# A gated linear attention feeding a gated state-space block: fourth group's alpha turned on VectorE, fourth block of the first projection moved ahead of the third group's scores

## The chip, the core and the metric

One core of a Trainium2 chip runs the whole program. Its engines work side by side and meet at semaphores: TensorE (PE in the profile; its weight loads are PEld), VectorE (DVE), ScalarE (ACT), GpSimd (POOL) and SyncE (SP), which here only issues transfers. Each engine works through its own instructions in the order in which they were written. The metric is the device time of one execution in microseconds; the kernel before takes 270.24 us in the median of three runs (270.16 to 270.40).

## What is computed

Two blocks, one feeding the other. The first is a gated linear attention over 4 batches, 8 heads, 768 steps and 48 channels. The second is a gated state-space block with 384 model channels and 512 inner ones.

```python
# first block, for each batch and head
for t in range(S):                       # S = 768
    state = alpha[t][:, None] * state + outer(k[t], v[t])
    y[t] = q[t] @ state
x = y.transpose(0, 2, 1, 3).reshape(4, 768, 384)

# second block
val, gate = split(x @ w_in)              # 512 and 512
h[t] = exp(A_log)[0] * h[t - 1] + val[t]   # along the steps, elementwise
out = (gate * sigmoid(gate) * h) @ w_out
```

## The kernel before, in words

**Groups.** The steps of a batch are cut into three groups of 256, so there are twelve groups, counted m or n = 0 to 11. The loop at the end of `fast` runs over n. In round n it makes the second block of group n (written with n) and the first block of group m = n + 1 (written with m), and it prepares q, k and alpha of the group behind that. Rounds 0 and 1 have an order of their own, written out by hand; from round 2 on the order repeats. The change lies in rounds 0 and 1. The schedule is manual: what stands first in the code is first on its engine.

**Turning q, k and alpha.** They come from memory with steps on the partitions and are needed with channels on the partitions. Two ways are in the code. `load_steps` fetches a group in two transfers, and `turned` then turns it on TensorE, either with a real transpose (L702, L703, for the groups and names in `turned_by_transpose`) or with a matmul against the identity (L707); ScalarE copies the result out of PSUM (`copy_turned`, L714; `alphas(m)` does all this for alpha). `load_raw` fetches a group in four transfers, arranged as squares of 32 partitions, and one VectorE instruction turns all of it (`turn`, L600). Groups 1 to 3 use the first way for alpha, later ones the second; q and k use the second from group 3 on. Both ways write into the same raw tile of each name: `load_steps` into one half of it by the parity of m, `load_raw` across both halves.

**First block of a group.** Turned alpha gives a running product P (L635) and its counterpart V (L654), two scans on VectorE over 1028 elements. `scaled_q` and `scaled_k` (L610, L619) multiply q by P and k by V. `scores` (L798) multiplies them on TensorE in blocks of 64 steps, `masks` (L808 for the first three groups, L813 later) puts the causal mask on them on VectorE and ScalarE copies the rest. `values` (L834) multiplies by v, `states` (L866) makes each block's contribution to the state, `add_banks` (L894) sums them on VectorE, `carried` (L847) adds what the state brings, and `join` moves the outcome into xT, the input of the second block: two ScalarE copies (L960, L961), eight small transfers half on SyncE's queue and half on GpSimd's (L963), and two ScalarE copies more (L966). `third(m)` is carried, values, carried, join.

**Second block of a group.** `project(n, cc)` is one of four blocks of the first projection: 128 value channels and 128 gate channels from xT and w_in (L988, twelve records on TensorE), a scan along the steps on VectorE (L995), and silu on ScalarE (L1006). It returns the product of the two as a function to be called later (L1008); with `late` the scan too is called later. `output` (L1022) is the second projection for groups 0 and 1.

**Weights.** w_in comes as four units, w_out as two halves, in 64-bit numbers. `load_w` and `load_w_out` fetch the bits on SyncE's queue. `low` (ScalarE, L543), `high` (VectorE, L549 and L551) and `add_low` (GpSimd, L556) turn them into 32-bit numbers; `convert` is all three. `load_w_out(0)` is issued behind a ScalarE instruction (L1218) that touches its buffer.

**PSUM.** Four banks (`mm0` to `mm3`) are handed out by `bank()` in the order of the string `taken`; every block of a projection, every second half of scores and every turned half takes from it.

**The order around the change.** Round 0 ends: block (0,2), with values and states of group 1 between its two halves; the load of w_out's first half; `alphas(3)`; `third(1)`; w_out's second half, q of group 3, alpha of group 4, v of group 3; the four scalings of group 2. Round 1 begins: scores and masks of group 2, block (0,3), the product of block (0,2), P of group 3, the scan of block (0,3), values and states of group 2, the products of blocks (0,0), (0,1), (0,3), block (1,0), both halves of w_out converted, block (1,1), the turn of k of group 3, `third(2)`, and so on.

Of the kernel before, what the change touches and what calls it, by code (L numbers as in the profile page):

```python
# [346 lines left out]
def fast(  # L347
# [22 lines left out]
    nc = tc.nc  # L370
# [24 lines left out]
    GP = GC + 1  # L395
# [6 lines left out]
    def load_raw(name, m, engine):  # L402
        if m >= N:
            return
        b, g = divmod(m, NG)
        src = srcs[name]
        to = raws[name][:, 0:4 * ROW].rearrange("p (h x) -> p h x", h=4)
        for i in range(2):
            for odd in range(2):
                n = ROW - 16 - 16 * odd  # L410
                engine.dma_start(
                    out=to[ds(64 * i + 32 * odd, 32), :, 0:n],
                    in_=src[b, ds(4 * i, 4), ds(g * GC, GC), :]
                    .rearrange("h (c j) d -> c h (j d)", c=32)[:, :, ds(32 * odd, n)])

    def steps_of(name, m):
        return raws[name][:, ds(m % 2 * (2 * ROW + 16), 2 * ROW + 16)]

    def load_steps(name, m, engines):
        b, g = divmod(m, NG)  # L420
        for i in range(2):
            engines[i % len(engines)].dma_start(
                out=steps_of(name, m)[:, ds(i * ROW, ROW)],
                in_=srcs[name][b, ds(4 * i, 4), ds(g * GC, GC), :].rearrange("h (c j) d -> c h (j d)", c=32))
# [34 lines left out]
    def load_w_out(half, engine):  # L459
        engine.dma_start(  # L460
            out=wobits[half].rearrange("p cc n two -> p cc (n two)"),
            in_=moe_w_out.bitcast(U32)[ds(2 * C * half, 2 * C)].rearrange("(cc p) n -> p cc n", p=C))
# [20 lines left out]
    als = [const.tile([C, 4 * GP + 1], FP32, name=f"al{i}") for i in range(2)]  # L483
# [74 lines left out]
    def convert(i):  # L558
        if i not in lows:
            low(i)  # L560
        high(i)
        add_low(i)
# [30 lines left out]
    def by_place(t):  # L593
        return t[:, 0:4 * GP].rearrange("p (h t) -> p h t", h=4)
# [4 lines left out]
    def turn(name, to):  # L599
        nc.vector.transpose(out=by_runs(to).rearrange("p h c j -> p h j c"),  # L600
                            in_=raws[name][:, 0:4 * ROW].rearrange("p (h j d) -> p h j d", h=4, d=D)
                            [:, :, :, 0:32])
# [58 lines left out]
    def products(m):  # L661
# [17 lines left out]

    taken = iter("0321032103231023" "1023102310231023" "102310231023" "10"
                 "23012301" "230132" "01230123" "012310" "23012301" "230132" "01230123" "012310"
                 "23012301" "230132" "01230123" "012310" "23012301" "230132" "01230123" "012310"
                 "23012301" "0132" "01320132")
# [6 lines left out]
    def bank_pair(tag=None):  # L692
        return [bank(tag and f"{tag}{i}") for i in range(2)]

    turned_by_transpose = ((0, "k"), (1, "a"), (1, "k"), (1, "q"), (3, "a"))

    def turned(m, name, js, t, by_transpose=None):
        raw = steps_of(name, m)
# [69 lines left out]
    def alphas(m):  # L768
        turn_over(m, "a", by_place(als[m % 2])[:, :, 1:GP])
# [17 lines left out]
    def scores(m, cs=range(G)):  # L787
        Zk, Zq = Zks[m], Zqs[m % 2]
        for c in cs:
            scs.setdefault(m, []).append(bank_pair(None if c else "s"))  # L790
            if not c or not m:
                sts.setdefault(m, []).extend(scs[m][c])
            for p in range(4):
                for h in range(2):
                    u = 2 * c + h
                    for i in range(2):
                        rows = ds(64 * i, D)
                        nc.tensor.matmul(scs[m][c][i][ds(L * h, L), ds(p * (L + D), L + D)],  # L798
                                         Zk[rows, c, p, ds(h * L, L)], Zq[rows, u, p],
                                         start=True, stop=True, skip_group_check=True)  # L800
# [351 lines left out]
    nc.scalar.activation(raws["a"][0:1, 0:1], sums[3][0:1, 0, 0:1], AF.Copy)  # L1152
    load_steps("a", 2, [nc.sync])
    load_w(units[2], nc.sync)
    for name in "kqa":
        load_steps(name, 2 + (name == "a"), [nc.sync])
    load_w(units[3], nc.sync)
    load_v(1, nc.sync)
    P = scan_P(1)
# [23 lines left out]
    def third(m):  # L1183
        if m < N:
            carried(m, (1,))
            values(m, False)
            carried(m, (0, 2, 3))
            return join(m, [nc.sync, nc.gpsimd])

    late = (1,)  # L1190
    for n in range(N):
        m = n + 1
        if n == 0:
# [14 lines left out]
            V = scan_V(2, P)  # L1208
            low(3)
            convert(3)  # L1210
            load_raw("k", 3, nc.sync)
            junk(1)
            def across_and_states():
# [3 lines left out]
            f2 = project(n, 2, between=across_and_states)  # L1217
            nc.scalar.activation(wobits[0][0:1, 0, 0, 0:1], minus[0:1], AF.Relu)  # L1218
            load_w_out(0, nc.sync)
            alphas(3)  # L1220
            third(m)
            load_w_out(1, nc.sync)
            for name in "qa":
                load_raw(name, 3 + (name == "a"), nc.sync)
            load_v(3, nc.sync)
            for c in range(G):
                scaled_k(2, tk, V, c)
                scaled_q(2, tq, P, c)
        elif n == 1:
            scores(m)  # L1230
            masks(m)
            h3, f3 = project(0, 3, True)
            f2()
            P = scan_P(3)
            h3()
            values(m, True)
            st = states(m)
            add_banks(m, st)
            for f in fs_late:
                f()  # L1240
            f3()
            f0 = project(n, 0)
            convert(4)
            junk(2)
            low(5)
# [11 lines left out]
            f2 = project(n, 2)  # L1257
# [4 lines left out]
            f3 = project(n, 3)  # L1262
# [6 lines left out]
        else:  # L1269
# [13 lines left out]
            f0 = project(n, 0)  # L1283
# [20 lines left out]
            f2 = project(n, 2)  # L1304
# [8 lines left out]
            f3 = project(n, 3)  # L1313
# [102 lines left out]
```

## Time and profile before

| | us |
|---|---|
| median of three runs (lowest, highest) | 270.24 (270.16, 270.40) |
| the profiled execution | 270.68 |
| its span | 269.0 |

The span is the stretch from the first to the last recorded instruction of one execution; every start time below counts from its beginning. In the chain of waits each row is a piece of the work that ended last, followed back from the end: start, length, engine, tile and line. In a timeline a row is a start, a length, an engine, a line, an operation with what it writes and reads, and in brackets how long the engine stood idle just before and what ended that. SPq is SyncE's queue: its rows are the issue of a transfer, and the rows with KB give the median time from issue to landing. Matmul durations overlap, so lengths on TensorE are taken from the chain, where pieces do not.

### The profile page before, as it was taken

Reading aid. Unit: us, or ns where it says so; the run is one execution under the profiler, and the core shown is the slowest. Engines: PE = TensorE matmul, PEld = TensorE weight load, DVE = VectorE, ACT = ScalarE, POOL = GpSimd, SP = SyncE. Lnnn points to the kernel's source line nnn. Section 1 sums busy time; section 2 is a strip of 40 time slices with the busy share of each in tenths; the row PEclk is TensorE's granted clock in tenths of the full one; section 3 lists DMA queues with packets and bytes.
Section 4 is the critical chain, followed back from the end, with each engine's and each line's share of the span. In section 5 each row is a group of like instructions: output and inputs, shape, how many; then the busy total and the mean of one; then the engine's idle time right before and its main releaser. Section 6 shows DMA issues by size and latency. Waiting matters only on the chain.

```text
span 269.0 us, 9976 instructions
## 1 busy us (share of the span) xinstructions
PE 263.0 (98%) x4168; PEld 230.2 (86%) x4168; DVE 233.5 (87%) x316; ACT 111.6 (41%) x270; POOL 165.3 (61%) x185
## 2 busy tenths in 40 slices
PE   7989999999999999999999999999999999999995
PEld 5978889886688988988988988988988989988974
DVE  7978898996999999999999999999999998883440
ACT  4666776281242631632543533524524515314011
POOL 8222304093267998996985995996886987646000
PEclk9999999999999999999999999999999999999999
DMA  5938974796993659559687478569588501201201
GB/s 173 316 117 281 296 172 139 210 225 159 243 220 90 138 159 231 119 140 229 133 227 170 107 207 184 113 173 219 128 210 172 144 3 29 75 3 37 70 7 59
DMA packets 52304, 41.19 MB, mean 153 GB/s; under 512 B 27392, under 2 KB 50944, under 8 KB 52256
## 3 DMA queue, kind: packets, MB, share of 16 engines
q1 hardware_dynamic: 49328, 37.34, 56.1%
q0 software_dynamic: 1536, 2.20, 3.1%
q10 hardware_dynamic: 1392, 0.99, 1.3%
q8 instruction: 34, 0.56, 0.9%
q14 instruction: 14, 0.11, 0.1%
HBM read 32.54 MB, written 4.72 MB: 139 GB/s over the span
## 4 chain that ended last, share of the span: by engine, by line
PE 96%; DMA 2%; issue 0%; ACTq 0%; ACT 0%
PE mm L988 48%; PE mm L1064 16%; PE y L834 4%; PE y L847 4%; PE mm L1022 4%; PE s L798 4%; PE mm L798 3%; PE s L866 3%; PE mm L707 2%; PE mm L1377 2%; DMA raw_q<-in_q_dram 2%; PE mm L702 2%; PE mm L703 1%; PE y L918 1%; PE mm L750 1%; PE y L926 1%
## 5 line engine op out<-in xcount | busy, mean ns | idle before, releaser
L988 PE MATMUL mm<-xT,w_in 128*128 128x256 f32 x576 | 129.4, 382 | 0.0
L988 PEld LDWEIGHTS mm<-xT,w_in 128*128 128x128 f32 x576 | 107.9, 190 | 16.0 <-issue 0.5
L1006 ACT ACTIVATE sg<-mm 128x256 f32<-128x256 f32 x48 | 18.4, 383 | 88.9 <-PE mm L988 88.9
L1008 POOL TENSOR_TENSOR f_last<-sg,hh 128x256 f32<-128x256 f32 x36 | 28.8, 806 | 26.1 <-ACT sg L1006 22.6
L886 POOL TENSOR_TENSOR sum<-sum,dS 128x192 f32<-128x192 f32 x30 | 39.3, 1310 | 3.0 <-ACT dS L874 1.4
L635 DVE TENSOR_TENSOR_SCAN P<-al,lower 128x1028 f32<-128x1028 f32 x12 | 30.5, 2541 | 0.3
L995 DVE TENSOR_TENSOR_SCAN hh<-a_dec,hh,mm 128x256 f32<-128x256 f32 x32 | 23.3, 728 | 8.4 <-PE mm L988 8.2
L654 DVE TENSOR_TENSOR_SCAN V<-al,ends 128x1028 f32<-128x1028 f32 x12 | 28.5, 2375 | 0.4
L963 POOL DMA_DIRECT2D xT<-yst x44 | 22.6, 518 | 5.4 <-ACT yst L960 4.0
L556 POOL TENSOR_TENSOR w_in<-w_in,wr 128x768 int32<-128x768 int32 x4 | 7.3, 1820 | 26.3 <-DVE wbits L1143 9.3
L1064 PE MATMUL mm<-wide,wr 128*128 128x192 f32 x108 | 20.8, 327 | 0.0
L600 DVE STREAM_TRANSPOSE k<-raw_k 128x1024 f32<-128x1024 f32 x9 | 18.5, 2053 | 0.0
L600 DVE STREAM_TRANSPOSE q<-raw_q 128x1024 f32<-128x1024 f32 x9 | 18.2, 2026 | 0.0
L1064 PEld LDWEIGHTS mm<-wide,wr 128*128 128x128 f32 x108 | 18.0, 190 | 0.0
L874 ACT ACTIVATE dS<-s 128x384 f32<-128x384 f32 (+1 forms) x18 | 7.4, 461 | 24.4 <-PE s L866 24.4
L818 POOL TENSOR_TENSOR AK<-AK,mask 128x512 f32<-128x512 f32 x9 | 13.7, 1520 | 5.9 <-ACT AK L814 5.7
L600 DVE STREAM_TRANSPOSE al<-raw_a 128x1024 f32<-128x1024 f32 x8 | 16.4, 2045 | 0.0
L619 DVE TENSOR_TENSOR Zk<-k,V 128x1024 f32<-128x1024 f32 (+1 forms) x14 | 15.8, 1128 | 0.1
L1064 PE MATMUL mm<-w_out,f_last 128*128 128x192 f32 x72 | 15.6, 339 | 0.0
L610 DVE TENSOR_TENSOR Zq<-q,P 128x1024 f32<-128x1024 f32 (+1 forms) x14 | 15.2, 1083 | 0.0
L847 PEld LDWEIGHTS y<-Zq,sum 48*64 48x64 f32 x656 | 11.6, 134 | 3.5 <-issue 3.0
L834 PE MATMUL y<-AK,v 64*64 64x64 f32 x352 | 14.5, 221 | 0.0
(188 smaller groups left out, 503.7 us busy)
## 6 DMA issues: line engine op xcount, KB each, us to landing
v<-in_v_dram SPq DMA_DIRECT2D x22, 192.0 KB, 3.6
out_dram<-o_sb SPq DMA_DIRECT2D x22, 192.0 KB, 2.7
raw_k<-in_k_dram SPq DMA_DIRECT2D x18, 184.0 KB, 4.6
raw_q<-in_q_dram SPq DMA_DIRECT2D x18, 184.0 KB, 4.7
raw_k<-in_k_dram SPq DMA_DIRECT2D x18, 176.0 KB, 4.9
raw_q<-in_q_dram SPq DMA_DIRECT2D x18, 176.0 KB, 4.7
wbits<-in_moe_w_in_dram SPq DMA_DIRECT2D x8, 384.0 KB, 5.7
raw_a<-in_alpha_dram SPq DMA_DIRECT2D x16, 184.0 KB, 3.6
```

The lines of the kernel that those rows point to most:

```text
L600: nc.vector.transpose(out=by_runs(to).rearrange("p h c j -> p h j c"), in_=raws[name][:, 0:4 * ROW].rearrange("p (h j d) -> p h j d", h=4, ...
L635: nc.vector.tensor_tensor_scan(out=P, data0=al[:, 0:4 * GP], data1=lower.rearrange("p h t -> p (h t)"), initial=0.0, op0=ALU.mult, op1=ALU ...
L654: nc.vector.tensor_tensor_scan(out=V[:, ::-1], data0=al[:, 1:4 * GP + 1][:, ::-1], data1=ends.rearrange("p h t -> p (h t)")[:, ::-1], init ...
L798: nc.tensor.matmul(scs[m][c][i][ds(L * h, L), ds(p * (L + D), L + D)], Zk[rows, c, p, ds(h * L, L)], Zq[rows, u, p], start=True, stop=True ...
L834: nc.tensor.matmul(ys[m][i][ds(64 * s, 64), e, ds(c * C + h * L, L)], v_sb[rows, c, 4 * i + p, :], As[i][rows, c, p, :], start=across and ...
L847: nc.tensor.matmul(ys[m][i][ds(64 * s, 64), e, ds(u * L, L)], Ss[j][rows, p, :], Zqs[m % 2][rows, u, p, D:], start=False, stop=True, skip_ ...
L886: nc.gpsimd.tensor_add(Ss[j][:, :, 0:D], Ss[j - 1][:, :, 0:D], part)
L963: engines[n % len(engines)].dma_start(out=xT[to, a], in_=st[rows, i, e])
L988: nc.tensor.matmul((pv, pg)[vg], w_ins[cc][:, kk, vg, :], xT[:, kk, :], start=(kk == 0), stop=(kk == NK - 1))
L995: nc.vector.tensor_tensor_scan(out=hh, data0=a_dec[:, cc:cc + 1].to_broadcast([C, GC]), data1=pv, initial=prev_h[cc][:, GC - 1:GC] if n % ...
L1008: f = lambda: engine.tensor_mul(fs[n][cc], sg, hh)
L1064: nc.tensor.matmul(o, a[:, k], b[k] if type(b) is list else b[:, k], start=start and k == 0, stop=k == KC - 1, skip_group_check=True)
```

## The change

It does three things together. Alpha of group 3 is fetched by `load_raw` and turned on VectorE by `turn` in round 1, between scores and masks of group 2, instead of fetched by `load_steps` and turned on TensorE in round 0; alpha of group 4, which takes the same raw tile, is fetched behind that turn. Block (0,3) of the first projection goes from behind the scores of group 2 to ahead of them, into round 0 behind `third(1)`; the product of block (0,2) and the scan of block (0,3) go ahead of the scores. Block (1,0) takes the place behind the masks, ahead of values and states of group 2. The string of banks has two entries fewer and its start is renamed to fit.

```diff
-    taken = iter("0321032103231023" "1023102310231023" "102310231023" "10"
+    taken = iter("3012301230102310" "2310231023102310" "2310231023" "10"
...
-    turned_by_transpose = ((0, "k"), (1, "a"), (1, "k"), (1, "q"), (3, "a"))
+    turned_by_transpose = ((0, "k"), (1, "a"), (1, "k"), (1, "q"))
...
     load_steps("a", 2, [nc.sync])
     load_w(units[2], nc.sync)
-    for name in "kqa":
-        load_steps(name, 2 + (name == "a"), [nc.sync])
+    for name in "kq":
+        load_steps(name, 2, [nc.sync])
     load_w(units[3], nc.sync)
...
             convert(3)
+            load_raw("a", 3, nc.sync)
             load_raw("k", 3, nc.sync)
...
             load_w_out(0, nc.sync)
-            alphas(3)
             third(m)
+            h3, f3 = project(n, 3, True)
             load_w_out(1, nc.sync)
-            for name in "qa":
-                load_raw(name, 3 + (name == "a"), nc.sync)
+            load_raw("q", 3, nc.sync)
             load_v(3, nc.sync)
...
         elif n == 1:
+            f2()
+            h3()
             scores(m)
+            turn("a", by_place(als[1])[:, :, 1:GP])
+            load_raw("a", 4, nc.sync)
             masks(m)
-            h3, f3 = project(0, 3, True)
-            f2()
+            f0 = project(n, 0)
             P = scan_P(3)
-            h3()
             values(m, True)
             st = states(m)
             add_banks(m, st)
             for f in fs_late:
                 f()
             f3()
-            f0 = project(n, 0)
             convert(4)
```

## The prediction, made before the changed kernel ran

> **What bounds the kernel now.** I read the page's span and busy shares first, then the chain of waits in order of time, then the timelines of the engines beside it.
>
> ```profile
> span 269.0 us, 9976 instructions
> PE 263.0 (98%) x4168; PEld 230.2 (86%) x4168; DVE 233.5 (87%) x316; ACT 111.6 (41%) x270; POOL 165.3 (61%) x185
> PE 96%; DMA 2%; issue 0%; ACTq 0%; ACT 0%
> ```
>
> The chain that ends last is 96% TensorE, so a microsecond taken off TensorE's order of work shortens the run, as long as nothing then arrives late. This is that chain over the stretch that the change rewrites (start, length, line, count):
>
> ```profile
> 40.88 0.11 PE mm L702
> ...
> 42.63 0.39 PE y L847 x16
> ...
> 44.19 0.77 PE s L798 x32
> 44.96 0.77 PE mm L798 x32
> 45.72 2.79 PE mm L988 x12
> 48.51 0.62 PE y L834 x32
> ...
> 49.84 5.38 PE mm L988 x24
> 55.22 0.39 PE y L847 x16
> ...
> 64.72 2.59 PE mm L988 x12
> 67.31 5.16 PE mm L1022 x16
> 72.47 0.93 PE s L798 x32
> ```
>
> Every piece starts where the one before it ends: TensorE waits for nobody here. From 40.88 to 42.63 it turns alpha 3 (L702 and L703); 45.72 is block 3 of group 0's projection, 49.84 blocks 0 and 1 of group 1's.
>
> **What goes.** The 16 transposes leave TensorE: 42.63 - 40.88 = 1.75 us. What follows them, the join's matmuls, keeps its 0.39 us start, since a 128-row matmul stands ahead of it either way (the piece at 55.22 has the same 0.39 behind the projection).
>
> **What moves.** The order becomes join work of group 1, block (0,3), scores, block (1,0), values and states, block (1,1). The same matmuls run, but the wide ones are no longer together. Two blocks in a row take 5.38 us, one alone behind small matmuls 2.79, so splitting them costs 2 x 2.79 - 5.38 = 0.20. Scores behind a wide matmul start with 0.93 instead of 0.77 (72.47 against 44.19): 0.16. **The sum on TensorE:** -1.75 + 0.20 + 0.16 = -1.39 us, if nothing is late.
>
> The new times on the old clock, from these lengths: join work 40.88 to 42.44; block (0,3) to 45.23; scores (0.93 + 0.77) to 46.93; block (1,0) to 49.72; values and states (49.84 - 48.51 = 1.33) to 51.05; block (1,1) to 53.84, where before it ended at 55.22. Now each input at its new time.
>
> VectorE and GpSimd, in their timelines:
>
> ```profile
> 39.79 1.82 POOL L556 TENSOR_TENSOR w_in<-w_in,wr 128x768 int32<-128x768 int32 x1 [6.21 <-DVE wr L551]
> 40.12 1.61 DVE L894 TENSOR_TENSOR sum<-s,sum 128x192 f32<-128x192 f32 x4
> 43.45 0.68 DVE L610 TENSOR_TENSOR Zq<-q,P 128x512 f32<-128x512 f32 x1
> 45.01 0.42 DVE L808 TENSOR_TENSOR A<-s,mask 128x256 f32<-128x256 f32 x1 [0.88 <-PE s L798]
> 54.12 4.25 POOL L556 TENSOR_TENSOR w_out<-w_out,wr 128x768 int32<-128x768 int32 x2 [6.93 <-ACT wr L543]
> 55.30 1.40 DVE L1008 TENSOR_TENSOR f_last<-sg,hh 128x256 f32<-128x256 f32 x1
> 66.06 0.75 DVE L995 TENSOR_TENSOR_SCAN hh<-a_dec,hh,mm 128x256 f32<-128x256 f32 x1 [2.50 <-PE mm L988]
> 70.14 0.41 DVE L1008 TENSOR_TENSOR f_last<-sg,hh 128x256 f32<-128x256 f32 x1
> 70.47 2.02 DVE L600 STREAM_TRANSPOSE al<-raw_a 128x1024 f32<-128x1024 f32 x1
> 72.34 2.04 DVE L600 STREAM_TRANSPOSE k<-raw_k 128x1024 f32<-128x1024 f32 x1
> ```
>
> Block (0,3) needs w_in 3, whose last addition ends at 39.79 + 1.82 = 41.61; its new start is 42.44, 0.8 us of room. The join work needs the sums, four additions of 0.4 us from 40.12: the first is there at 40.5 (wanted 40.88), the third at 41.3 (wanted at about 42.2).
>
> VectorE's added turn of alpha 3 costs 1.87 us, by the distance of the two turns at 70.47 and 72.34. It is hidden by idle time. VectorE now waits 0.88 us before the masks and 2.50 us before the scan of block (1,3), and for nothing that the profile shows between them. New: it comes out of the scaling at 44.13, takes the product of block 2 (about 0.4) and the scan of block (0,3) (0.66) at once, then the turn, then four masks of 0.36, until 48.4. TensorE wants the masks at 49.72, 1.3 us later. The stretch from 45.01 to 63.56 (66.06 less the wait of 2.50) is 18.55 us long; begun at 44.13 and lengthened by 1.87 it ends at 64.55. The scan behind it could start at 66.06 - 1.39 = 64.67. So the added work fits to a tenth of a microsecond, and the wait of 2.50 us is used up. Behind it there is room once more: the product at 70.14 ends at 70.55, while the last quarter of the output projection that reads it begins 12/16 into the 5.16 us from 67.31, at 71.18. That 0.6 us would not shrink. GpSimd's two additions for w_out, from 54.12 to 58.37, wait for VectorE too: its part for them comes up to 1.87 - 0.88 = 0.99 later, so they end between 58.37 and 59.36. The first output projection starts at 64.72 - 5.16 = 59.56, now 1.39 sooner at 58.17, and reads the second half of w_out in its third product of eight, 4/16 of 5.16 later, at 59.46: 0.1 to 1.1 us of room. I cost all this at nothing; without the two idle stretches the turn would be 1.87 us on the path.
>
> The rest of the moved block is its silu on ScalarE and its scan. They free its pair of PSUM banks for block (1,0) by about 45.7 (45.23 and a product's 0.4), before 46.93.
>
> ScalarE loses two copies of al and gains nothing but order. SyncE's queue and the transfers:
>
> ```profile
> 25.05 1.18 SPq L422 DMA_DIRECT2D raw_a<-in_alpha_dram  x2
> 28.00 5.82 SPq L441 DMA_DIRECT2D v<-in_v_dram  x4
> 34.85 1.91 SPq L411 DMA_DIRECT2D raw_k<-in_k_dram  x4
> raw_k<-in_k_dram SPq DMA_DIRECT2D x2, 184.0 KB, 3.5
> DMA packets 192, 0.24 MB, mean 245 GB/s; under 512 B 21, under 2 KB 192, under 8 KB 192
> 41.41 0.39 SPq L460 DMA_DIRECT2D wobits<-in_moe_w_out_dram  x1
> wobits<-in_moe_w_out_dram SPq DMA_DIRECT2D x1, 768.0 KB, 4.5
> 44.86 3.17 SPq L963 DMA_DIRECT2D xT<-yst  x4
> 47.45 0.58 SPq L963 DMA_DIRECT2D xT<-yst  x1
> xT<-yst SPq DMA_DIRECT2D x1, 48.0 KB, 1.9
> 57.50 4.85 SPq L963 DMA_DIRECT2D xT<-yst  x4
> L963 POOL DMA_DIRECT2D xT<-yst x44: 501/510/544, 45.1 to 247.5; - x44
> ```
>
> The two early loads of alpha 3 (2 x 192 KB, 25.05) go, so what stands behind them, w_in 3 and v, is issued 1.2 us sooner. In their place four square loads (2 x 184 + 2 x 176 = 720 KB) are issued ahead of raw_k, from about 32.6. With the time of raw_k's own squares, 3.5 us, doubled for the v packets in front, they land before 41; the turn wants them at 45.1. The bytes grow by 336 KB, 1.4 us at the 245 GB/s that the queue moved from 38 to 39, and the queue stands still between raw_k's landing (the last of four issues starts at about 36.3, and 3.5 more: 39.8) and 41.41. The load of alpha 4 moves behind v 3 and behind the turn at 47; its reader turns at 70.47, now about 69: covered by 15 us. Behind its wait in SyncE's queue stand only the moves of the next join (57.50).
>
> The one input that comes nearer is **xT of group 1**. Now SyncE's last move for it starts at 47.45 and lands at 49.35; TensorE started on it at 49.84 and needs the last third of it 0.20 + 2 x 0.43 = 1.06 later. In the new order the join work ends 1.75 us earlier, so do the copies, and the moves, if nothing holds them: landing at 47.6. Block (1,0) starts at 46.93 and needs the last third at 47.99. Room 0.4 us, where it was 1.5. What could hold them is the load of the first half of w_out, 768 KB, issued at 41.41 as now and landed at 45.9: the first move would be issued 1.7 us behind it instead of 3.45. Bounds: nothing lost, or the landing at 49.35 as before, 1.36 us lost. The nearest row is the next join at 57.50, with four issues in 4.85 us instead of 3.17: the first at 44.86 - 1.75 = 43.11, the last starting at 43.11 + 4.85 - 0.58 = 47.38, and 1.9 to land give 49.3 too. I take nothing lost: w_out's load ends at 45.9, and SyncE's four moves hold 128 KB, 0.5 us of the queue at 245 GB/s, so that even all behind it they fit before 47.99.
>
> **The sum.** The profiled execution took 270.68 us with a span of 269.0: new 270.68 - 1.39 = 269.29, span 267.6. It lies 0.44 above the median of the runs, 270.24; from that median 268.85.
>
> **The rivals.** *xT late (B).* The moves wait behind the w_out load and land near 49.35: up to 1.36 us is given back, 268.85 to 270.2, the middle 269.5. For it: the row at 57.50. Against it: the moves are 48 KB and less, and the load ends at 45.9.
>
> *VectorE the bound (C).* The fit to a tenth above breaks when products run beside GpSimd's additions: one more 1.40 us product in place of 0.41, less the 0.1 or 0.6 us of room, costs 0.4 to 0.9: 269.5. Against it: the stretch already holds one such product (55.30).
>
> [...]
>
> *The queue backs up, slower than before (D).* All on SyncE's one queue: if v does not come sooner, 720 KB of squares at 245 GB/s push raw_k's landing from 39.8 to 42.7. The w_out load, issued at 41.41, then moves 1.3 us later and lands at 47.2, the moves of xT come through behind it with the 3.17 us of their four issues, at about 50.4, and block (1,0) stands for 50.4 - 47.99 = 2.4 us: 1.0 us slower, 271.25. It turns the sign once the last move lands after 47.99 + 1.39 = 49.4. For it: v's four issues took 5.82 us, the queue was full there. Against it: the quiet from 39.8 to 41.4, and 384 KB that no longer stand in front.
>
> **How the numbers follow.** Forecast 0.60, B 0.17, C 0.09, L 0.03, D 0.11. The predicted time is 268.85, its own range 268.5 (the whole 1.75 without the boundary costs) to 269.4. The range reaches through most of B: 268.4 to 270.3. This kernel's measurement tells about 0.2% from no change, 0.54 us: faster is below 269.70, which holds nearly all of the forecast, half of B and most of C, 0.75; within 0.2%, the rest of B, L, and edges of C and D, 0.14; slower, D, 0.11.
>
> **What would show it.** Right: no transposes of alpha after group 2; join work starting at about 40.9; block (1,1) ending near 53.8, with pieces that meet; the scan of block (1,3) with no more than some tenths of idle time before it; the scores behind the second output at 71.1. Wrong: a gap on TensorE inside block (1,0) with xT's moves named (B, D; D also has w_out's landing past 46.5), a gap before values with the masks named, a gap in the output projection with w_out or a VectorE product named (C), a GpSimd issue of a move above 0.6 us (L). A gain beyond 1.75 us would mean that something earlier than 40 us moved, which no step here explains.

## The result, and the profile after

The changed kernel takes 281.98 us in the median of six executions (280.47 to 285.72); the kernel before, on the same chip, 270.02 (269.73 to 270.40). The ratio is 1.044, 95% interval 1.038 to 1.050: 12 us slower, where 1.4 faster was forecast. Each ratio in this text compares the means of the executions within 1.5% of their kernel's fastest one, while a median counts all executions. The profiled execution of the changed kernel is the longest of its six, 285.72 us; its head and its row of waits on TensorE follow. The waits' columns are the total, the number and the longest, in microseconds; "issue" means that the profile shows nothing that TensorE waited for.

```profile
span 284.0 us, 9942 instructions
PE 268.3 (94%) x4152; PEld 233.7 (82%) x4152; DVE 240.1 (85%) x317; ACT 110.9 (39%) x268; POOL 158.9 (56%) x185
PEclk9999997999999999799999999999799999999999
q8 instruction: 33, 0.54, 0.8%
PE 69%; DVE 19%; issue 6%; DMA 3%; ACT 1%; POOL 1%; DVEq 0%; ACTq 0%; POOLq 0%
```

```profile
PE mm L798 <- issue: 2.6, 1, 2.6
PE mm L988 <- DVE hh L995: 2.3, 1, 2.3
PE mm L1064 <- issue: 2.3, 1, 2.3
PE mm L988 <- issue: 1.9, 1, 1.9
PE mm L1064 <- DVE A L813: 1.3, 1, 1.3
PE y L779 <- PEq L1401: 1.0, 1, 1.0
PE y L847 <- POOL sum L886: 0.5, 1, 0.5
```

The 16 transposes are gone (4168 matmuls before, 4152 now), yet TensorE is busy for 268.3 us instead of 263.0, and its share of the chain fell from 96 to 69%. "issue", 0% of the chain before, is 6%. The granted clock, 9 tenths or more in all 40 slices before, dips in three. (The wait of 1.0 us at L779 is the start of the run and stands in the kernel before too.) The same stretch of the chain of waits as in the prediction shows the first loss:

```profile
40.52 0.39 PE y L847 x16
40.91 0.47 PE y L834 x32
41.38 0.70 PE y L847 x48
42.08 0.41 PE mm L988
42.49 1.90 issue
44.39 4.22 PE mm L988 x11
48.61 0.93 PE s L798 x32
49.54 0.77 PE mm L798 x32
50.30 2.79 PE mm L988 x12
...
54.42 2.79 PE mm L988 x12
```

The join work starts at 40.5 (about 40.9 in the forecast), the scores take 0.93 + 0.77, the two split blocks 2.79 each. But block (0,3) starts its first matmul and then stops for 1.90 us with nothing named, and its other eleven take 4.22 us instead of 2.38. The same pair stands at two more places in the full chain:

```profile
114.86 1.78 issue
116.63 6.28 PE mm L1064 x28
...
197.85 2.56 issue
...
201.03 6.43 PE mm L1064 x28
...
222.22 4.75 PE mm L1064 x28
```

The 28 matmuls of L1064 take 4.75 us in an undisturbed round and 6.28 or 6.43 behind a gap. Why they are slow stands in the busy time by stretch (PE busy, PEld, DVE, ACT, POOL, then the granted clock, the transfers' share and GB/s):

```profile
42.50:44.40 1.90, 0.01 (x1) 0.01 (x1) 1.90 (x4) 1.34 (x4) 1.39 (x3) 1.00 0.83 306
44.40:48.60 4.20, 4.20 (x15) 3.13 (x15) 2.03 (x3) 0.00 (x0) 0.67 (x2) 0.59 0.81 234
201.00:207.50 6.50, 6.50 (x38) 6.27 (x38) 5.02 (x5) 3.06 (x9) 2.21 (x3) 0.74 0.36 72
```

In the gap nothing runs on TensorE, and the stretch behind it is granted 0.59 and 0.74 of the clock. So each of these three gaps costs twice, itself and 4.63 - 2.79 = 1.84, 6.28 - 4.75 = 1.53 and 6.43 - 4.75 = 1.68 us of slow matmuls. In this trace the clock is at half for 3.41 us each time, from 44.56, from 116.24 and from 201.57 on; the first of these begins behind only 1.9 us of idle time, the row at 42.5.

The account against the forecast's span of 267.6: 284.0 - 267.6 = 16.4 us. The six waits listed, without the one at L779, are 10.9, the three slow stretches 5.05, together 15.95.

**What TensorE lacked.** The page's q8 carries instructions: 33 packets and 0.54 MB, 16 KB each. TensorE's matmuls, weight loads and the rest are 8409 records, some 255 to a packet (34 packets and 8442 records in the kernel before), so I take a packet for a block of 256, an estimate from these counts. Counted in the trace, the gaps begin with TensorE's record 1728, 3776 and 6336, whatever stands there (a projection, an output, scores): 6.75, 14.75 and 24.75 times 256. A fourth long one, at 157, begins with 5056, 19.75 times. The transfers of the kernel before from 39.6 to 41 us, all of them:

```profile
DMA packets 1, 0.02 MB, mean 12 GB/s; under 512 B 0, under 2 KB 0, under 8 KB 0
q8 instruction: 1, 0.02, 4.5%
```

Those of the kernel after from 38.3 to 41.8, without a packet of q8,

```profile
DMA packets 589, 0.75 MB, mean 215 GB/s; under 512 B 65, under 2 KB 589, under 8 KB 589
q1 hardware_dynamic: 589, 0.75, 102.5%
```

then from 41.8 to 43.4:

```profile
q1 hardware_dynamic: 101, 0.28, 59.4%
q8 instruction: 1, 0.02, 4.6%
```

And SyncE's issues ahead of that, in its timeline (720 KB in each row):

```profile
33.34 2.66 SPq L411 DMA_DIRECT2D raw_a<-in_alpha_dram  x4
36.11 1.80 SPq L411 DMA_DIRECT2D raw_k<-in_k_dram  x4
```

In the kernel before, the block of instructions moves at 39.66, as k 3's squares run out. In the kernel after, the queue is full of squares, alpha 3's and then k 3's, and the block moves at 41.89. Such a packet, but for a program's last, starts at the soonest 0.81 us (kernel before) and 0.87 us (after) behind the moment at which TensorE has passed 0.55 of a block; I call that moment "asked for". It is an estimate from these earliest starts, since the trace has no record of the request.

| kernel, first block | asked for | packet starts | lag | records run out | running again |
|---|---|---|---|---|---|
| before | 38.60 | 39.66 | 1.06 | no gap | |
| after | 38.23 | 41.89 | 3.66 | 42.49 | 44.39 |

The records in hand lasted 42.49 - 38.23 = 4.26 us in the new order, and TensorE ran again 2.50 us behind the packet's start. In the old order the transposes stood among the same records, 32 of them for 1.75 us, and TensorE came to record 1728 only at 43.73, 5.1 us behind the request. So theory **A**: the new order uses up the records in hand sooner, a lag above about 4.26 - 2.5 = 1.8 us stops TensorE, and the added squares make the lag. The 33 records fewer shift every later block's end into other work, where the loads of the repeating rounds do the same. **B'** is the rival: the gaps come with the change itself, its order, waits and banks.

### The profile page after: what moved, and what is told of

Same layout as the page of the kernel before. It is cut to its first block, busy times and chain, and to the rows that moved or that the text cites. A ratio compares the mean times of both kernels' runs of the same rounds, so it can differ in the third digit from the quotient of the medians.

```text
span 284.0 us, 9942 instructions
## 1 busy us (share of the span) xinstructions
PE 268.3 (94%) x4152; PEld 233.7 (82%) x4152; DVE 240.1 (85%) x317; ACT 110.9 (39%) x268; POOL 158.9 (56%) x185
## 4 chain that ended last, share of the span: by engine, by line
PE 69%; DVE 19%; issue 6%; DMA 3%; ACT 1%; POOL 1%; DVEq 0%; ACTq 0%; POOLq 0%
PE mm L988 36%; PE mm L1064 15%; PE y L834 3%; PE y L847 3%; DVE P L635 3%; DVE al L600 3%; DVE V L654 3%; PE mm L798 2%; PE s L866 2%; DVE q L600 2%; PE s L798 2%; PE mm L1378 2%; PE mm L1022 2%; DMA v<-in_v_dram 1%; DVE hh L995 1%
## 5 line engine op out<-in xcount | busy, mean ns | idle before, releaser
L988 PE MATMUL mm<-xT,w_in 128*128 128x256 f32 x576 | 131.4, 387 | 4.3 <-DVE hh L995 2.3
L988 PEld LDWEIGHTS mm<-xT,w_in 128*128 128x128 f32 x576 | 109.2, 192 | 20.8 <-DVE hh L995 2.9
L1064 PE MATMUL mm<-wide,wr 128*128 128x192 f32 x108 | 22.9, 351 | 0.0
L1064 PEld LDWEIGHTS mm<-wide,wr 128*128 128x128 f32 x108 | 20.2, 209 | 0.0
L1064 PE MATMUL mm<-w_out,f_last 128*128 128x192 f32 x72 | 16.7, 358 | 3.6 <-issue 2.3
L600 DVE STREAM_TRANSPOSE al<-raw_a 128x1024 f32<-128x1024 f32 x9 | 18.4, 2044 | 0.0
L818 POOL TENSOR_TENSOR AK<-AK,mask 128x512 f32<-128x512 f32 x9 | 11.5, 1281 | 9.4 <-ACT AK L814 9.3
L619 DVE TENSOR_TENSOR Zk<-k,V 128x1024 f32<-128x1024 f32 (+1 forms) x14 | 16.7, 1192 | 0.1
L1064 PEld LDWEIGHTS mm<-w_out,f_last 128*128 128x128 f32 x72 | 12.7, 204 | 4.9 <-issue 4.0
```

The lines of the kernel that those rows point to most:

```text
L619: nc.vector.tensor_mul(Zks[m][:, ds(c0, n)].rearrange("p c h t -> p h c t"), t[:, :, at].rearrange("p h (c t) -> p h c t", t=C), V[:, :, 1 ...
L988: nc.tensor.matmul((pv, pg)[vg], w_ins[cc][:, kk, vg, :], xT[:, kk, :], start=(kk == 0), stop=(kk == NK - 1))
L1064: nc.tensor.matmul(o, a[:, k], b[k] if type(b) is list else b[:, k], start=start and k == 0, stop=k == KC - 1, skip_group_check=True)
```

## The experiments

The theories' expectations stand as they were written before each run.

**1. Put the 33 records back, or take as many away from the kernel before.** Small transposes that write a bank which nobody reads, behind the first output projection: 16 of them (with their weight loads 32 records) in the kernel after, 112 in the kernel before.

```diff
             output(0)
+            pad = bank("s0")
+            for _ in range(16):
+                nc.tensor.transpose(pad[0:32, 0:32], ident[0:32, 0:32], ident[0:32, 0:32])
             sum_weights()
```

> The changed kernel with 16 transposes of 32x32 zeros-or-ones more on TensorE behind the first output projection, into a PSUM bank that nobody reads; they compute nothing that is used. They put every later TensorE instruction back to the place in the stream of 16,384-byte instruction blocks that it has in the kernel before. Theory A (TensorE runs dry at block ends, and where the ends fall decides): the gaps put down to issue near 114, 157 and 198 us go, with their half-speed clock windows of 3.4 us; the gap at 42 us (in front of the padding) and the wait for VectorE near 67 us stay: 272 to 276 us against 281 to 282. Theory B (the squares of alpha 3, 720 KB, crowd the transfer queue, and the rest follows from the lateness): the padding changes nothing, 280 to 283 us.

> The kernel before with 112 such transposes at the same place: its later TensorE instructions then stand in the blocks as those of the changed kernel do (224 instructions more, 33 fewer, are the same place modulo 256, to a few). The transposes themselves take 1.5 to 3 us of TensorE. Theory A: the gaps of the changed kernel near 114, 157 and 198 us appear in a kernel that has nothing of the change, each 2 to 4.5 us with its half-speed window: 275 to 284 us. Theory B: 270 us and the price of the transposes, 271.5 to 273 us, no gap put down to issue of more than 1 us after 60 us.

Measured: the kernel after with the 16 takes 273.74 us (ratio to the kernel before 1.0125, 1.0067 to 1.0182), 8 us less with more work. Every long gap behind the padding is gone. So is the 2.3 us wait for VectorE, which was expected to stay: in the kernel after's profile one conversion of w_out's bits (L551, at 58.38) takes VectorE 2.22 us, with the padding 0.61, and the trace does not show why. The gap ahead of the padding stays, in its chain:

```profile
40.23 0.39 PE y L847 x16
...
41.78 0.41 PE mm L988
42.20 2.70 issue
44.90 4.00 PE mm L988 x11
...
57.50 0.39 PE y L847 x16
```

The kernel before with the 112 takes 282.0 us (1.0465, 1.0406 to 1.0523). Its profiled span is 278.7 us, 9.7 above the 269.0 of the kernel before. The padding itself is 3.4 of them. Another 1.7 is the block behind the padding, which takes 4.47 us instead of 2.79 from 67.21 on, without a gap (the whole execution was granted 0.988 of the clock). The rest is gaps that the kernel before never had, at 113 and 156 (3.4 us in two; the third that was expected, near 198, is not there), and 1.4 us of slow matmuls behind the first, in its chain:

```profile
112.47 0.76 PE mm L798 x31
113.23 2.04 issue
```

That gap begins with record 4032, 15.75 times 256. Both say A: gaps come and go with the count of records, with and without the change. The padding also shifts what follows by 0.57 or 3.4 us; that the gaps begin at the same remainder of 256 in the kernel after, in this one and in k late (experiment 3) is what speaks for the count and against the mere shift.

**2. Each half of the change alone.** The move without alpha 3's new way (its diff against the kernel before), and alpha 3's new way with the old order of blocks, the reverse of these lines in the kernel after.

```diff
             third(m)
+            h3, f3 = project(n, 3, True)
             load_w_out(1, nc.sync)
...
+            f2()
+            h3()
             scores(m)
             masks(m)
-            h3, f3 = project(0, 3, True)
-            f2()
+            f0 = project(n, 0)
             P = scan_P(3)
-            h3()
...
-            f0 = project(n, 0)
```

> The kernel before with the move of the blocks alone: block (0,3) ahead of the scores, block (1,0) behind the masks, alpha 3 still turned on TensorE. As many TensorE instructions as before, and later ones at the same place in the blocks. Theory A: no new gap after 60 us; the two added changes between wide and small matmuls cost 0.36 us: 270.2 to 271 us. Theory C (the move itself starves a later stage): 274 us or more.

> The kernel before with alpha 3 alone fetched as squares and turned on VectorE between scores and masks; blocks (0,3) and (1,0) stay where they were. 32 TensorE instructions fewer. Theory A: gaps put down to issue after 100 us as in the changed kernel, 274 to 283 us. Theory B: a gap at 42 us and no others: 270 to 274 us. Theory C: 268.5 to 270 us, since the move is left out.

Measured: the move alone 271.89 us (1.0072, 1.0037 to 1.0107), no issue gap in its profile, 1.4 us above the 0.36 that its two boundary costs would make and above the 270.2 to 271 expected. The one profiled execution (span 270.1, 1.1 above the kernel before's) shows 0.6 us as a wait for GpSimd's sums at 88 us; where the rest is it does not show. Alpha alone 280.33 (1.029, 1.0228 to 1.0353), with gaps of 1.3 to 2.6 us at 43, 112, 156 and 197. It removes the 33 records and adds the squares, and it has 8 of the 12 us by the ratio, 10 by the medians.

**3. The queue alone, not one instruction of TensorE moved.** k 3's squares behind w_out's second half; or, from round 2 on, q's squares behind the scores, just ahead of v; the second also in the kernel before.

```diff
             load_raw("a", 3, nc.sync)
-            load_raw("k", 3, nc.sync)
...
             load_w_out(1, nc.sync)
+            load_raw("k", 3, nc.sync)
```

```diff
             go(1)
-            load_raw("q", n + 3, nc.sync)
...
+            load_raw("q", n + 3, nc.sync)
             load_v(m + 2, nc.sync)
```

> The changed kernel with the four square loads of k 3 issued behind the load of w_out's second half (about 46 us) instead of right behind those of alpha 3; k 3 is turned at 57 us or later. Theory A, now in two parts (a fetch of TensorE's instructions waits for what the transfer queue already holds, and TensorE runs dry where it uses up the 256 instructions in hand sooner): the fetch that started at 41.9 us starts before 40.5, the gap at 42 us and its half-speed window go, about 4 us less: 276 to 278.5 us; the gaps after 100 us stay. Rival (the gap at 42 comes from where the block ends alone): the gap stays, 280 to 283 us.

> The changed kernel with, from round 2 on, the four square loads of q issued behind the scores of the next group, just ahead of v, instead of ahead of block 3 of the projection. No TensorE instruction moves, so block ends fall as in the changed kernel. Theory A: fetches asked for in the join work and the scores no longer find 720 KB in front, the gaps near 114, 157 and 198 us go: 272 to 275 us with the gap at 42 left. Rival (block ends alone decide, whatever the queue holds): 280 to 283 us.

> The kernel before with q from round 2 on issued behind the scores, nothing else. It has no gap after 60 us that this could remove. Theory A: 269.5 to 270.6 us, no difference. Rival (loading q later is a gain of its own, apart from the gaps): below 269.2 us.

Measured: q late 275.56 us (1.0235, 1.0186 to 1.0284): the gaps near 111, 152 and 193 are 0.7 us or less, that at 42 stays (2.09, here with a granted clock of 1.0 over the whole execution). k late 279.16 (1.0206, 1.015 to 1.0262): the gap at 42 is gone (lag 1.22), the later ones stay (1.5 to 2.8 us), and a new one of 2.58 us stands at 56, record 2240, 8.75 times 256, whose block lagged by 5.12 us behind k 3, q 3, v 3 and alpha 4. In the kernel before the same edit changes nothing, 270.49 (1.0012, 0.9986 to 1.0038). So what a load costs depends on which block's request it stands ahead of.

**4. Clearing several places at once.** k and q late together; k late with the 16 transposes; then also q 3 and alpha 4 behind the join of group 2 ("spread"), and w_out's first half behind the join of group 1; last, alpha 3's squares themselves put off until that join. "Spread" differs from the kernel with both late by

```diff
             load_raw("k", 3, nc.sync)
-            load_raw("q", 3, nc.sync)
             load_v(3, nc.sync)
...
-            load_raw("a", 4, nc.sync)
...
             third(m)
+            load_raw("q", 3, nc.sync)
+            load_raw("a", 4, nc.sync)
             load_raw("k", 4, nc.sync)
```

and "alpha 3 late", where q 3 and alpha 4 come behind block (1,1) and v 3 behind the join of group 2, from the one with q late by

```diff
-            load_raw("a", 3, nc.sync)
             load_raw("k", 3, nc.sync)
...
-            load_w_out(0, nc.sync)
+            load_raw("a", 3, nc.sync)
             third(m)
+            load_w_out(0, nc.sync)
```

> Both moves of loads on the changed kernel. Theory A: no gap put down to issue above 1 us anywhere, no half-speed window before the end; what is left is the sum of the prediction, -1.39 us: 268.2 to 269.6 us, below the kernel before. Rival (VectorE is now the bound near 67 us): a wait for a scan there, 270 to 272 us.

> The changed kernel with k 3 late and the 16 padding transposes of the first set, q as in the changed kernel. Theory A: no gap at 42 us, none after 100 us, 0.57 us for the padding: 268.9 to 270.2 us. Rival: as the changed kernel with padding alone, 272 to 276 us.

> The changed kernel with its loads spread so that few of them are queued when TensorE asks for instructions ahead of a dense stretch: k 3 behind w_out's second half, q 3 and alpha 4 behind the join work of group 2, q from round 2 on behind the scores. Theory A: none of the gaps near 42, 56, 111, 152 and 193 us is above 1 us, no half-speed window; the wait of about 1.0 us for xT at 46 us, which the two kernels with k 3 late showed, stays: 270.0 - 1.39 + 1.0 = 269.6 us, 269.0 to 270.4. Rival (the gaps come back at other block ends whatever is spread): 272 us or more.

> The same with the load of w_out's first half issued behind the join work of group 1, so that xT's moves find nothing in front. Theory (rival B of the prediction: the w_out load holds the moves): the wait at 46 us goes, 268.3 to 269.4 us. Rival: w_out, k 3 and v then stand together in the queue and a fetch near 51 us comes late: 271 us or more.

> The kernel after, with its loads in another order: the squares of k 3 at their place, those of alpha 3 behind the first transposes, w_out's two halves behind the two scores of round 1, those of q 3 and alpha 4 behind block (1,1), q's from round 2 on late. Theory (TensorE's instruction blocks wait behind queued loads): the block asked for at about 38 us finds only k 3's 240 KB ahead of it, as in the kernel before, and comes about 1 us later; the block asked for at about 50.6 finds only the rest of w_out. So no issue gap of TensorE above 1 us, no stretch at half the clock, a wait for xT of 0 to 0.5 us, and 268.6 to 270.0 us. Rival (the join and the scores are too dense for one block in hand, whatever is queued, or the loads put off are late at another place): an issue gap of 1.4 us or more at 42 or 55, or a wait for alpha 3 or xT of 1 us, and 271.5 us or more.

| | us, ratio | long waits of TensorE left |
|---|---|---|
| k and q late | 274.03, 1.0155 (1.0108 to 1.0202) | issue 1.8 at 56, xT 1.0 (listed as ACT K, see 5) |
| k late, 16 transposes | 275.19, 1.0158 (1.0116 to 1.0201) | issue 3.1 at 55, xT 0.9 |
| spread | 272.72, 1.0098 (1.0063 to 1.0134) | issue 1.4 at 55 and 0.7 at 110, xT 0.8 |
| spread, w_out later | 273.8, 1.0115 (1.008 to 1.0151) | issue 2.1 at 55 and 0.8 at 112 |
| alpha 3 late | 273.86, 1.0133 (1.0092 to 1.0173) | xT 2.4, issue 0.9 at 113 |

All five missed: none came below the kernel before. Each cleared or shortened a place that it was made for and left or gave another; "spread" was made for the gap at 56 too and still has 1.4 there. In "alpha 3 late" the block asked for at 38.37 came after 1.22 us and 42 has no gap, as expected; but the 720 KB (k 3's squares too are 720 KB, not the 240 of the expectation) stood ahead of xT's moves, whose row in its profile says so:

```profile
DMA to landing us min/median/max: 5.2/5.4/6.0
```

2.0 in the kernel before. Its profiled execution is one of its longer ones, 276.06 us. w_out's place told the same from the other side: with its first half behind the join, xT's wait was gone and the block that TensorE lacked at 55 came 4.67 instead of 4.47 us after it was asked for.

**5. Alpha 3's squares loaded before that stretch.** A buffer that is free by 30 us, that of the first weights' bits, takes them where v 2 was loaded; these kernels' line numbers are 5 higher from there on. They share

```diff
+    def raw_of(name, m):
+        if (name, m) != ("a", 3):
+            return raws[name]
+        return wbits[units[0]].rearrange("p kk vg n two -> p (kk vg n two)").bitcast(FP32)
...
-    load_v(2, nc.sync)
+    load_raw("a", 3, nc.sync)
...
             convert(3)
-            load_raw("a", 3, nc.sync)
```

with q 3's and alpha 4's squares behind block (1,1), v 3 behind the join of group 2, q late, and one small fill of the buffer's padding on GpSimd. They differ in three loads:

| | behind convert(3) | ahead of the join of group 1 | behind it |
|---|---|---|---|
| early | k 3 (720 KB) | w_out 0 (768 KB) | w_out 1, v 2 (384 KB) |
| early, w | k 3 | none | w_out 0, w_out 1, v 2 |
| early, v | k 3 | v 2 | w_out 0, w_out 1 |
| early, k | v 2 | k 3 | w_out 0, w_out 1 |
| early, x | v 2 | none | w_out 0, w_out 1, and k 3 at 51 us |

> The kernel after with alpha 3's squares (720 KB) in a buffer of their own (that of the first weights, which are turned by then), loaded at about 30 us where v 2 (384 KB) was loaded; v 2 behind w_out's second half; k 3's squares at their place, so that they are all that the block asked for at about 38 us finds ahead of it, as in the kernel before; q 3's and alpha 4's behind block (1,1), v 3 behind the join of the third group, q's from round 2 on late. The theory (the change's arithmetic on TensorE holds; all that was lost is instruction blocks and xT behind queued loads): no issue gap of TensorE above 1 us, a wait for xT of at most 0.4 us as forecast, no stretch at half the clock, 268.4 to 269.8 us. The rival (the arithmetic fails too, or the room of some other transfer is used up wherever the squares go): no such gap and 270.2 us or more, or another wait of 1 us or more (for xT, for v 2, or for the block at 50.6 us) and 271.5 us or more.

> As the one with alpha 3's squares early, but the first half of w_out behind the join of the second group, so that xT's moves have only k 3's squares ahead of them and the block asked for at about 50.6 us more of w_out. The theory: xT's wait is gone (0.4 us less than there, if there is any), and the block at 50.6 comes later by what is more in front of it (384 to 768 KB, 1.5 to 3 us): 268.4 to 269.8 us if it still comes within 4 us of being asked for, else an issue gap of 1 to 2 us at about 55 us and 271 to 273 us. The rival: xT is as late as there, since w_out was not what held it.

> As the one with alpha 3's squares early and w_out's first half behind the join of the second group, but v 2 (384 KB) ahead of that join, where w_out's first half stood: only k 3's squares ahead of the block asked for at about 38 us, half as much as there ahead of xT, and v 2 in time. The theory (what was lost is blocks and inputs behind queued loads, the arithmetic holds): no issue gap of TensorE above 1 us, no wait for v 2 or xT above 0.4 us, no stretch at half the clock; what is left are gaps under 1 us at about 109 and 189 us and VectorE's 0.3 us: 268.6 to 270.0 us, less than the kernel before in the same call. The rival (the arithmetic fails too, or another transfer is late): the waits are gone and the time is 270.3 us or more, or a wait of 1 us or more stands at another place and it is 271.5 us or more.

> As the one with v 2 ahead of the join of the second group, with v 2 (384 KB) and the squares of k 3 (720 KB) in each other's places, so that the block asked for at about 38 us has 336 KB less ahead of it (some 1.2 us at the 280 GB/s that these loads moved at) than the 2.97 us that it waited there. The theory: that block starts at about 39.8 to 40 us instead of 40.99, the issue gap of 1.1 us at 42 us is gone or below 0.3 us, xT is on time behind the 720 KB as it was behind w_out's 768 KB, and the time is 0.6 to 1.2 us below that kernel's best executions (270.67 to 271.3): 269.3 to 270.3 us, at or below the kernel before. The rival (this stretch has no room for the squares anywhere): the gap stays within 0.3 us of 1.1, or a wait of 0.5 us or more for xT or for k 3's keys, or a gap at another block's end takes its place, and 270.7 us or more.

> As the one with v 2 and k 3 in each other's places, with k 3's squares behind block (1,0), at about 51 us, so that nothing stands ahead of xT's moves. The theory (the 1.2 us before block (1,0)'s matmuls there was xT behind 720 KB, its moves landing after 4.2 us instead of 2.0): the moves land after 2 to 2.6 us, the wait of 1.2 us is gone, no issue gap above 0.4 us at 42 or 55, and the profiled execution falls from 270.4 to about 269.2 us, below the kernel before; the median, with executions that still lose a block somewhere, 268.9 to 270.2. The rival (another input becomes the last one: k 3's keys, VectorE's turn of them, w_out's additions): a wait of 0.5 us or more with one of them named, and 270.3 us or more.

| | median (lowest), ratio | profiled execution, span | block asked for at 38: lag, gap | other waits above 0.4 |
|---|---|---|---|---|
| early | 273.18 (272.33), 1.0111 (1.0083 to 1.0138) | 273.21, 271.5 | 2.55, 1.10 | v 2 1.1, issue 0.5 |
| early, w | 277.52 (276.14), 1.026 (1.023 to 1.029) | 277.17, 275.5 | 1.43, none | v 2 3.9, issue 0.7 and 0.5 |
| early, v | 273.71 (270.67), 1.0097 (1.0064 to 1.013) | 270.86, 269.1 | 2.97, 1.11 | none |
| early, k | 273.93 (270.39), 1.0131 (1.0086 to 1.0177) | 270.39, 268.7 | 1.06, none | xT 1.2 |
| early, x | 274.5 (270.58), 1.0101 (1.0066 to 1.0137) | 274.37, 272.7 | 1.22, none | VectorE 2.5, issue 0.6, q at the start 0.6 |

The chain of "early, v" is the cleanest view of the forecast's own steps, with one short gap in it:

```profile
40.30 0.39 PE y L852 x16
...
41.86 0.41 PE mm L993
42.27 1.11 issue
43.38 2.53 PE mm L993 x11
...
54.51 0.39 PE y L852 x16
```

"Early, k" then showed that this gap too was a block behind k 3's squares: with 336 KB less in front the lag is 1.06 instead of 2.97 and the gap is gone (the 280 GB/s of the expectation is high: "early, v" moved 235 from 34 to 38 us). Its one wait is listed as

```profile
PE mm L993 <- ACT K L815: 1.2, 1, 1.2
```

and that name is wrong. "Early, x", with nothing ahead of xT's moves, has the wait down to 0.28, and there block (1,0) starts ahead of that copy:

```profile
46.33 1.89 PE L993 MATMUL mm<-xT,w_in 128*128 128x256 f32 x6 [0.28 <-DVE al L605]
46.48 0.33 ACT L815 ACTIVATE K<-s 128x192 f32<-128x192 f32 x1 [1.71 <-DVE A L813]
```

So it was xT: in the trace of "early, k" its first two moves land at 46.66 and 46.87, and the block starts at 47.01. They stood behind k 3's squares:

```profile
DMA to landing us min/median/max: 3.8/4.2/4.7
```

"Early, x" failed by the rival's first case: k 3's squares landed late, and VectorE stood for them:

```profile
59.39 2.04 DVE L605 STREAM_TRANSPOSE k<-raw_k 128x1024 f32<-128x1024 f32 x1 [2.06 <-DMA raw_k<-in_k_dram]
```

No version beat the kernel before: the medians of the last three are 3.3 to 4.1 us above it, though their best executions, 270.39 to 270.67, are within 0.3 us of it. Their executions spread over some 5 us, while the 17 of the kernel before beside "early, x" spread over 2.0 and those beside "early, v", with two long ones, over 4.7. Which block or load is late in the long ones can't be said, since each kernel has one profile; that the lag of a block varies from one execution to the next would explain it, and stays an argument.

## Why the prediction was wrong

**The sum on TensorE was right.** From the start of the join work to the end of block (1,1) the prediction has 53.84 - 40.88 = 12.96 us, before it was 55.22 - 40.88 = 14.34. "Early, v" took 54.51 - 40.30 = 14.21; less the gap of 1.11 and the 0.15 by which block (0,3) is longer around it (0.41 + 2.53 - 2.79), 12.95. The kernel after with 16 transposes took 57.50 - 40.23 = 17.27; less 2.70 and 1.62, 12.95. So the sum of -1.75, +0.20 and +0.16 holds to a hundredth. The span of "early, k" less that one wait, 268.7 - 1.2 = 267.5, is near the forecast's 267.6; it is the shortest of that kernel's six executions, so part of the agreement is luck.

**The step that failed is "if nothing is late".** "TensorE waits for nobody here" is true of the kernel before, and the prediction carried it over to the new order by a list of inputs (w_in 3, sums, masks, xT, w_out) that left out TensorE's own instructions: their late blocks were put at nothing and cost gaps of 1.3 to 2.6 us. The 1.75 us that the transposes took were also the time in which the next block of instructions came. A lag costs nothing while the 300 or so records in hand last, and without the transposes these last 4.26 us instead of 5.1. Every gap at 42 fits one rule, lag plus about 2.5 us against 4.26: lags of 1.06 ("early, k"), 1.22 (k late, alpha 3 late, "early, x") and 1.43 ("early, w") gave none, 2.55 ("early") gave 1.10, 2.97 ("early, v") 1.11, 3.66 (after) 1.90, 3.81 (q late) 2.09, 4.22 (after with 16 transposes) 2.70.

**"The 16 transposes leave TensorE" was counted as time alone.** That 33 records fewer move the end of each later block was no term of the sum. It was the largest one: putting the records back gives back 8 us (experiment 1). The queue is the other half of it, since moving q's loads alone gives back 6 (experiment 3).

**D had the cause and not the victim.** It saw 720 KB of squares in SyncE's queue and priced xT at 2.4 us through w_out's landing. In the kernel after w_out was issued at 41.05, as before, and xT was on time, since block (0,3) itself had stood. The queue hit the instruction block.

**B was real, once nothing hid it.** With the gap at 42 gone, xT was late by 0.8 to 1.2 us behind w_out or k 3, and by 2.4 behind alpha 3. The step that took "nothing lost" argued from bytes, 0.5 us for 128 KB; the moves' landing of 4.2 and 5.4 us shows that they wait for far more than their own bytes.

**VectorE and the rest.** The added turn of alpha 3 fitted: in "early, v" no wait above 0.2 us names VectorE. In the kernel after's profile two waits do. The one of 2.3 us follows the slow conversion of experiment 1, whose cause stays open. The one of 1.3 us, at 157, is the gap that begins with record 5056; TensorE runs again 2.58 us behind the packet at 156.14, as in the other gaps, so its name is probably wrong. With the 16 transposes both are gone, so C did not decide. No run shows L, a GpSimd issue of a move above 0.6 us, which had 0.03 of the chances: these take 501 to 542 ns in the kernel after and, from 40 to 50 us, 501 to 539 in "early, v" and "early, k".

## What to carry to other kernels

In these kernels TensorE's own instructions were an input like any other: where many short instructions stand close together, ask how long some 300 of them last (4.26 us here, and a lag of 3.66 us stopped TensorE for 1.90) and what has just been put into the transfer queue (720 KB of squares here). The gaps named "issue" that began at the same remainder of 256 records each time were that input being late, and taking 33 records out made this kernel slower far behind the place of the edit (1.78 us at 115, 2.56 at 198). Test it by padding the count of records, or by moving one load, before anything else is believed of the change.

## What the runs showed of the hardware that was not expected

A block, by the estimate of 256 records one packet of 16,384 bytes in the trace, starts moving at best 0.81 us (kernel before) and 0.87 us (after) after TensorE passes 0.55 of the block before, and takes 0.88 to 1.79 us in these two. At the four long gaps of the kernel after, all of them with squares in the queue, it started 2.60 to 5.09 us after it was asked for, and TensorE ran again 2.50 to 2.72 us behind its start; at the new gap of k late the lag was 5.12 us. In the kernel before, with 34 such packets, TensorE has one "issue" wait, of 0.8 us in 270; in the kernel after the three issue waits alone are 6.8 us.

The clock did not fall behind every gap. In the kernel after the stretches at half clock last 3.41 us each and begin at 44.56, 116.24 and 201.57, 21 and 25 times 3.41 us apart. In the 3.41 us ahead of them TensorE ran no matmul for 1.90, 1.87 and 2.25 us. In two others of the same length, from 65.04 (a share of the wait of 2.3 us) and from 157.20 on, it ran none for 1.68 and 1.32 us, and the clock behind both was 1.0. The execution of "early, v", with its gap of 1.11 us, was granted 1.0 throughout, and so was that of q late with 2.09. Three stretches look different: in alpha alone the matmuls are slow from 44.38 to 50.05, and in "early, w" from 53.17 into the block at 55.90, which takes 4.29 us instead of 2.79, longer than 3.41 us in both; and in the kernel before with 112 transposes the slow block at 67.21 has the small transposes ahead of it and no gap.
